# A new order of all engines' work and of all PSUM banks in a fused attention and mixture-of-experts kernel

## The chip, the cores and the metric

The kernel runs on one core of a Trainium2 chip. The metric is the device time of one execution in microseconds. Five engines work side by side, each in its own program order: TensorE (PE: matmuls, transposes; its weight loads are listed apart as PEld), VectorE (DVE), ScalarE (ACT), GpSimd (POOL) and SyncE (SP). They wait for each other through semaphores. Transfers run on 16 DMA engines and are issued here from the queues of GpSimd (the rows' loads), SyncE (stores, small constants) and ScalarE (one weight).

## The reference

Local attention over 8 batches, 8 heads, 576 positions and 64 values per head. Heads 0 to 3 see the last 32 positions, heads 4 to 7 every fourth of the last 128. The result, as 4608 tokens of 512 values, goes through a gated pair of low-rank experts.

```python
scores = scale * np.matmul(q, k.transpose(0, 1, 3, 2))
mask_plain = (rel >= 0) & (rel < 32)
mask_dil = (rel >= 0) & (rel < 128) & (rel % 4 == 0)
attn = softmax(where(mask, scores, -1e9))
x = (attn @ v).transpose(0, 2, 1, 3).reshape(4608, 512)
...
logits = x @ w_gate                     # 8 experts, the best 2 of each token
w = softmax(the two logits)
out = x + sum over the 2 experts of w * ((x @ A[e]) @ B[e])   # rank 16
```

## The kernel before

The host lays q, k and v out so that the dilated heads become plain bands as well (positions sorted by their remainder of 4), and ones are put beside v so that the softmax's sums come out of the same matmul. One batch is one "row", r = 0 to 7; g = 0 are the plain heads, g = 1 the dilated ones.

For each row, in names that the plan uses (a digit for the part, then r, then g):

- **Loads** L, on GpSimd's DMA queue, from f32 to bf16 on the way, into four input slots (row r uses slot r % 4, so row r waits until row r-4 has been used). Rows 2 to 6 are one operation of two DMAs each. Rows 0, 1 and 7 are cut up: Lq7gh are the queries and keys of one group and half, Lv7gh its values.
- **S0, S1** (TensorE): masks, then scores of key blocks 0 to 4 and 5 to 8, 24 and 20 matmuls, into two banks each. **E0, E1** (ScalarE): exponentials into the tile p.
- **V** (TensorE, 26 matmuls, three banks): the values. **R** and **N** (VectorE): reciprocal of the sums and the product with it, into the row x. **B** (GpSimd): x as bf16.
- **T**, **U** (TensorE): transposes of it, **C**, **Cd**, **Cp** (ScalarE) their copies to xt. **Z0, Z1** (TensorE): x times A and the gate, **Y0, Y1** (ScalarE) copies.
- **m0, m1, s12, tt, top, g2** (VectorE) and **th** (ScalarE): the gate's weights from the two largest logits. **gz** (GpSimd, VectorE in row 7): gated products. **G**, **H** (TensorE): their transposes; **gc**, **gn** (ScalarE) copies.
- **D0, D1, D2** (TensorE): products with B. **A0, A1, A2** (VectorE) add them to x; in the last rows a part goes by ScalarE (**dx**, **dy**) and GpSimd (**A3**, **A2**).
- **O** (SyncE): the row's store. Rows 6 and 7 are stored in halves. Every store waits for six of the eight loads of row 7 (Lq700, Lq701, Lq710, Lq711, Lv710, Lv711), and a store of a whole row for the one two before it in the plan.

At the start stand warm and the fillers F0 to F2 (matmuls on a tile of zeros), awf/awc and btf/btc (weights and their casts), con, cc0, cc1 and cd0 to cd3 (the masks), tab (a first exponential), pz, xz and vz (fills with zeros).

The order of everything is a text, PLAN. A word is an operation's name; after an @ stands the first of the PSUM banks that it takes. `Program.ordered` reads it: each engine executes its operations in the order in which they stand there, and an operation that takes a bank waits for all that last used this bank. `Program.run` makes the semaphore waits from these and from the dependencies named in `add(...)`. Neither looks at times.

## Time and profile before

| | |
|---|---|
| median of 3 runs | 101.61 us (101.57 to 102.17) |
| the profiled execution | 101.74 us, span 100.0 us |
| busy in the span: PE, PEld, DVE, ACT, POOL | 81.0, 59.3, 61.6, 72.0, 51.0 us |
| HBM read, written | 29.07 MB, 9.44 MB |
| matmuls | 1585, with as many weight loads |
| mean granted TensorE clock | 0.974 of full speed |

The span goes from the first to the last instruction of the program. In a row of the timeline stand start, length, engine, line, operation, written and read tiles, count, and in brackets the idle time before it and what ended that. A row of the chain has start, length and what. A row of windows has a stretch, its length, busy time and count of PE, PEld, DVE, ACT and POOL, the granted clock, the share of the DMA engines' time and their rate. A row of groups ends with busy time, mean nanoseconds of one, idle time before. "issue" is time in which an engine waited for nothing that the profile shows.

### The profile page before, as it was taken

To read this page: it belongs to the slowest core of one execution; us is meant where nothing else is said; L and a number is where in the kernel's file an instruction comes from. 1 tells how busy PE (TensorE), PEld (TensorE's weight loads), DVE (VectorE), ACT (ScalarE), POOL (GpSimd) and SP (SyncE) were. 2 spreads that over 40 slices of the span, in tenths; PEclk is the share of its full clock that TensorE was granted. 3 is DMA by queue.
4 is the path that set the end of the run, shared out by engine and by line. 5 is a ranking of instruction groups with operands and counts; after the bars stand their busy time and mean duration, and the time that the engine had idled before them with its cause. 6 is when DMAs were issued, how large, how long until landed. Compare 5 with 4: busy or idle time off the path is not lost.

```text
span 100.0 us, 3591 instructions
## 1 busy us (share of the span) xinstructions
PE 81.0 (81%) x1585; PEld 59.3 (59%) x1585; DVE 61.6 (62%) x138; ACT 72.0 (72%) x123; POOL 51.0 (51%) x68
## 2 busy tenths in 40 slices
PE   5999979969874886989886996999999999868300
PEld 3345565547554664669654865887886888745100
DVE  5800068732991458908926498297597399989700
ACT  5643740998986977795699488979989999956300
POOL 5999006915440050852960346749367508666800
PEclk9999999999999999999999999999999999999955
DMA  2999999999999999999999999797889999869994
GB/s 47 310 207 200 213 211 212 223 202 214 213 210 222 209 214 209 213 219 212 213 210 218 209 212 216 127 214 138 153 198 424 428 405 417 364 269 420 420 415 168
DMA packets 5727, 24.50 MB, mean 245 GB/s; under 512 B 720, under 2 KB 848, under 8 KB 4944
## 3 DMA queue, kind: packets, MB, share of 16 engines
q0 software_dynamic: 3840, 14.23, 72.1%
q1 hardware_dynamic: 1728, 9.77, 23.7%
q10 hardware_dynamic: 144, 0.28, 0.9%
q8 instruction: 12, 0.20, 0.8%
q14 instruction: 3, 0.02, 0.1%
HBM read 29.07 MB, written 9.44 MB: 385 GB/s over the span
## 4 chain that ended last, share of the span: by engine, by line
PE 48%; DMA 21%; ACT 13%; DVE 5%; POOL 4%; issue 3%; POOLq 0%
PE ps L212 43%; DMA in<-in_qkv_dram 21%; ACT p L345 8%; PE ps L408 3%; PE ps L498 2%; DVE x L384 1%; POOL x L553 1%; DVE x L545 1%; DVE tt L483 1%; POOL xb L391 1%; ACT xt L418 1%; ACT gn L517 1%; ACT awf L571 1%; POOL x L573 1%; ACT gc L514 1%
## 5 line engine op out<-in xcount | busy, mean ns | idle before, releaser
L345 ACT ACTIVATE p<-ps 128x960 bf16<-128x960 f32 (+1 forms) x32 | 27.7, 891 | 7.6 <-PE ps L212 7.1
L391 POOL CAST xb<-x 128x1152 bf16<-128x1152 f32 (+1 forms) x16 | 17.6, 1111 | 22.0 <-DVE x L384 22.0
L212 PE MATMUL ps<-in,p 128*64 128x130 bf16 (+1 forms) x416 | 21.4, 221 | 1.5 <-ACT p L345 1.5
L384 DVE TENSOR_TENSOR x<-ps,rec 128x1152 f32<-128x1152 f32 x16 | 21.7, 1357 | 0.5
L212 PEld LDWEIGHTS ps<-in,p 128*64 128x64 bf16 (+1 forms) x416 | 17.1, 104 | 4.7 <-ACT p L345 2.1
L545 DVE TENSOR_TENSOR x<-x,ps 128x1024 f32<-128x1024 f32 (+1 forms) x16 | 17.3, 1114 | 1.2 <-PE ps L212 1.2
L381 DVE RECIPROCAL rec<-ps 128x18 f32<-128x18 f32 x16 | 4.3, 271 | 21.8 <-PE ps L212 21.5
L493 POOL TENSOR_TENSOR gz<-zs,g 128x640 bf16<-128x640 f32 x7 | 8.9, 1274 | 16.5 <-DVE g L488 16.5
L212 PE MATMUL ps<-warm 128*128 128x512 f32 x20 | 11.9, 738 | 1.2 <-DVE warm L216 1.2
L272 POOL DMA_DIRECT2D in<-in_qkv_dram x22 | 11.7, 570 | 0.8 <-POOLq L674 0.8
L212 PEld LDWEIGHTS ps<-in 64*64 64x64 bf16 x576 | 10.7, 106 | 2.4 <-issue 0.4
L212 PE MATMUL ps<-in 64*64 64x96 bf16 (+1 forms) x576 | 11.6, 200 | 0.2 <-issue 0.2
L212 PE MATMUL ps<-aw,xt 128*128 128x136 bf16 x160 | 11.2, 223 | 0.7 <-ACT xt L424 0.4
L418 ACT COPY xt<-ps 128x1024 bf16<-128x1024 bf16 x8 | 8.1, 1011 | 4.0 <-PE ps L408 4.0
L408 PE MATMUL ps<-one,xb 128*128 128x128 bf16 x128 | 9.6, 219 | 1.6 <-issue 0.9
L212 PEld LDWEIGHTS ps<-aw,xt 128*128 128x128 bf16 x160 | 9.6, 98 | 1.5 <-ACT xt L424 0.7
L408 PEld LDWEIGHTS ps<-one,xb 128*128 128x128 bf16 x128 | 7.6, 98 | 3.1 <-issue 1.4
L466 ACT COPY zs<-ps 128x408 f32<-128x408 f32 (+1 forms) x14 | 6.1, 443 | 3.3 <-PE ps L212 3.1
L212 PEld LDWEIGHTS ps<-warm 128*128 128x128 f32 x20 | 4.4, 239 | 5.6 <-issue 4.3
L212 PE MATMUL ps<-bt,gc 128*128 128x256 bf16 (+1 forms) x48 | 6.7, 256 | 1.2 <-ACT gc L514 0.7
L421 ACT COPY xt<-ps 128x1024 bf16<-128x1024 bf16 x7 | 7.2, 1022 | 0.6 <-PE ps L408 0.6
L212 PE MATMUL ps<-con,one 64*64 64x480 bf16 (+1 forms) x64 | 5.9, 359 | 2.1 <-DMA in<-in_qkv_dram 1.7
(54 smaller groups left out, 98.1 us busy)
## 6 DMA issues: line engine op xcount, KB each, us to landing
in<-in_qkv_dram POOLq DMA_DIRECT2D x10, 868.5 KB, 17.9
out_dram<-x SPq DMA_DIRECT2D x6, 1152.0 KB, 5.8
in<-in_qkv_dram POOLq DMA_DIRECT2D x10, 288.0 KB, 5.6
out_dram<-x SPq DMA_DIRECT2D x4, 576.0 KB, 3.6
in<-in_qkv_dram POOLq DMA_DIRECT2D x10, 146.2 KB, 7.3
in<-in_qkv_dram POOLq DMA_DIRECT2D x2, 434.2 KB, 13.2
awf<-in_aw_dram ACTq DMA_DIRECT2D x1, 272.0 KB, 3.0
btf<-in_bt_dram SPq DMA_DIRECT2D x1, 256.0 KB, 3.3
```

The lines of the kernel that those rows point to most:

```text
L212: return nc.tensor.matmul(o, lhsT=lhsT, rhs=rhs, start=start, stop=stop, skip_group_check=True)
L272: nc.gpsimd.dma_start(out=IN[r % SLOTS][half(a), at : at + n], in_=qkv[r, a, :, at - 2 * VB * a : at - 2 * VB * a + n],) if n < ROW else n ...
L345: return [nc.scalar.activation(p[:, :, :].rearrange("p h (s c) -> p h s c", c=PER)[:, :, b0 : b0 + nb, 0:SEG], PS[:, k.at : k.at + 2, 0 : ...
L381: rc = add(f"R{tag}", "DVE", ("el", 60), lambda: [nc.vector.reciprocal(rec[:, :].rearrange("p (b i) -> p b i", b=3), PS[:, k.at : k.at + 3 ...
L384: nm = add(f"N{tag}", "DVE", ("el", XG), lambda: [nc.vector.tensor_tensor(X[r][:, XG * g : XG * g + XG].rearrange("p (b i n) -> p b i n", ...
L391: add(f"B{tag}", "POOL", ("el", cut), lambda: [nc.gpsimd.tensor_copy(XB[r % 2][:, g, 0:cut], X[r][:, XG * g : XG * g + cut])], [nm] + free)
L408: nc.tensor.transpose(tp[j][:, 128 * u : 128 * u + 128], xb[:, g, 256 * u + 128 * j : 256 * u + 128 * j + 128], ident())
L418: return [nc.scalar.copy(xt[:, 0:2, 0:S].rearrange("p j (c i) -> p j c i", c=C)[:, :, :, 0:128], tp.rearrange("p j (i c) -> p j c i", c=C))]
L421: return [nc.scalar.copy(xt[:, 2:4, 0:512], tp)]
L466: zc.append(add(f"Y{st}{r}", "ACT", ("el", len(us) * ZW), lambda us=us, k=k: [nc.scalar.copy(zs[:, us[0] : us[-1] + 1].rearrange("p u n -> ...
L493: return [en.tensor_tensor(GZ[i][:, us[0] : us[0] + n, :].rearrange("p u (e r) -> p u e r", e=E), zv()[:, us[0] : us[0] + n, 0:ER].rearran ...
L545: return [nc.vector.tensor_tensor(v, v, PS[:, k.at : k.at + nk].rearrange("p b n -> p (b n)"), ALU.add)]
```

## The change

PLAN is replaced by another order of the same 426 operations with other banks, and the waits of the first copies on ScalarE name tab (which stands before them on the same engine) as well. All operations, their shapes and the rest of their dependencies stay; so does the wait of the stores for six of row 7's eight loads. The new order is the result of a search in which TensorE's instruction fetches were counted.

```diff
-    add("cc0", "ACT", ("el", SEG), ..., ["con"])
+    add("cc0", "ACT", ("el", SEG), ..., ["con", "tab"])
...
-        CON[:, 3 * SEG :]..., ONE[:, 0:SEG]...)], ["con"])
+        CON[:, 3 * SEG :]..., ONE[:, 0:SEG]...)], ["con", "tab"])
...
-                    zeros(i, a).bitcast(FP), WARM[...]...)], ["wz"])
+                    zeros(i, a).bitcast(FP), WARM[...]...)], ["wz", "tab"])
```

The text before:

```
con awf btf wz tab cc0 pz1 pz0 Lk00 cc1 vz21 vz00 Lk01 xz0
vz01 warm@7 cd3 Lv00 xz1 cd2 S100@1 pz3 cd0 Lv01 L11 S000@5 E000 F0@4
btc cd1 L10 E100 S001@6 S101@4 V00@1 E101 awc L2 E001 V01@5 R00 F1@0
N00 B00 T00@4 C00 R01 F2@3 N01 B01 U0@6 Cp0 Cd0 T01@7 C01
L3 L4 S111@2 S011@0 Z00@7 E011 Y00 Z10@0 vz10 vz11 Y10 pz2 m00 m10
s120 E111 S110@6 S010@4 top0 tt0 th0 g20 E110 gz0 E010 V11@0 R11 N11
G0@7 V10@3 B11 R10 gc0 N10 gn0 D02@7 D00@0 B10 A02 T11@6 vz20 D01@2
vz30 C11 U1@7 Cd1 Cp1 T10@4 A00 C10 S121@0 E121 A01 Z11@2 Y11 m11
Z01@7 Y01 S021@5 m01 top1 E021 S020@3 S120@1 s121 tt1 th1 g21 gz1 E020
V21@5 E120 G1@3 R21 gn1 V20@0 gc1 N21 D12@3 R20 D11@6 vz31 A12 N20
S030@4 B20 E030 D10@0 S130@2 E130 S131@4 E131 B21 A11 A10 S031@6 E031 L5
U2@0 T21@5 V30@1 Cd2 T20@4 R30 C21 N30 B30 V31@5 Cp2 R31 N31 L6
C20 Z12@0 Y12 Z02@1 Y02 m02 m12 s122 S141@2 E141 S140@5 E140 T30@7 S041@1
tt2 th2 E041 B31 U3@0 S040@5 C30 V41@1 Cd3 Cp3 top2 g22 gz2 G2@0
E040 gn2 gc2 R41 N41 T31@4 V40@5 D22@3 R40 A22 N40 C31 Z03@0 Z13@2
Y03 m03 Y13 S150@3 m13 s123 D20@0 E150 S151@6 E151 S051@4 D21@2 top3 tt3
th3 B41 B40 A20 T41@7 E051 g23 A21 gz3 U4@1 T40@0 C41 Lq700
Lq711 Lq701 S050@2 Lv710 Cp4 V51@5 R51 N51 Cd4 G3@1 E050 V50@2 R50 N50
C40 gn3 Z14@0 gc3 B51 Y14 Z04@5 Y04 S060@0 B50 D30@6 E060 S160@4 Lq710
E160 Lv711 Lv701 S161@2 E161 D32@1 Lv700 A30 T50@0 S061@6 A32 C50 m14 m04
top4 V60@1 s124 tt4 T51@4 th4 U5@0 E061 V61@5 O0 R60 N60 O1 S170@2
Cp5 g24 C51 Cd5 Z05@1 E170 R61 Z15@4 Y05 Y15 gz4 N61 G4@0 B60
gn4 D31@6 m05 gc4 B61 S070@2 E070 S171@4 A31 m15 T60@0 top5 E171 s125
tt5 th5 g25 S071@6 O2 O3 V70@1 R70 T61@4 E071 C60 V71@5 U6@0 N70
C61 Cp6 D42@1 Cd6 dx4 gz5 G5@4 D40@2 Z06@1 A42 R71 N71 gn5 gc5
A40 D41@6 A41 B70 Bx7 Y06 Z16@4 Y16 m06 D52@0 dx5 U7@1 B71 Cd7
T70@2 m16 O4 s126 Cp7 T71@3 C70 D50@0 A52 top6 D51@5 tt6 Cx7 th6
C71 Z07@2 Z17 g26 A50 A51 gz6 dy5 m07 G6@7 gc6 m17 s127 tt7
th7 top7 A53 O5 g27 gz7 gy7 D61@0 gn6 A61 D62@5 dx6 A62 O61
D60@6 dy6 A63 G7@2 H7 gn7 D70@5 gc7 gm7 D72@3 dx7 A72 A60 O60
D71@1 A70 A71 D73@6 dy7 A73 O71 O70
```

The text after:

```
awf wz con warm@5 awc F0@4 btf btc Lk00 pz3 tab cc0 S100@0 cc1
Lk01 cd1 S000@5 Lv00 vz20 vz01 vz00 vz10 pz1 cd2 cd3 F1@7 xz1 vz30
Lv01 vz21 L11 L10 vz11 pz0 pz2 E100 E000 L2 cd0 S001@3 E001 S101@0
E101 V00@5 R00 N00 V01@2 B00 T00@7 R01 C00 S111@0 S011@5 N01 B01 U0@3
T01@2 Cp0 C01 Cd0 xz0 Z00@2 E111 E011 Z10@7 Y00 m00 S010@3 Y10 m10
S110@5 V11@0 top0 s120 tt0 E010 R11 th0 E110 g20 L3 N11 V10@3 R10
N10 gz0 B11 G0@6 gn0 T11@7 gc0 D00@0 A00 F2@2 vz31 B10 U1@6 C11
Cd1 T10@2 S020@0 Cp1 C10 E020 S121@5 E121 D01@2 Z11@4 Y11 A01 L4 Z01@1
Y01 m01 S120@5 S021@3 D02@7 A02 E120 E021 V20@0 m11 top1 s121 tt1 th1
g21 R20 V21@3 N20 gz1 G1@0 gc1 R21 N21 B20 S130@1 gn1 E130 S131@3
D11@6 A11 S030@1 E131 B21 S031@3 E030 T21@5 V30@0 R30 T20@6 U2@7 N30 C21
E031 V31@3 R31 N31 C20 Cp2 Cd2 Z12@1 Y12 Z02@0 Y02 D10@6 A10 S141@2
E141 S140@4 L5 m02 E140 S041@0 E041 S040@6 B30 m12 s122 tt2 th2 T30@3
E040 D12@2 A12 B31 T31@4 L6 top2 U3@5 Cp3 g22 V41@0 Cd3 C31 C30
R41 N41 gz2 V40@5 G2@4 gc2 gn2 Z13@3 R40 N40 Z03@2 Y03 m03 Y13
m13 D20@0 Lq711 B41 A20 Lq710 s123 B40 Lv711 S150@6 E150 S051@2 D21@4 A21
E051 S151@6 E151 S050@0 E050 tt3 th3 T41@2 C41 top3 V51@3 g23 gz3 R51
N51 B51 T40@7 U4@6 C40 V50@0 Cp4 Cd4 G3@7 R50 Z14@3 gc3 gn3 Y14
Z04@5 T51@4 Y04 N50 D30@6 Lq701 Lq700 B50 C51 S160@0 S060@2 A30 m04 E160
S161@4 S061@6 E060 D22@0 m14 top4 E161 s124 A22 Lv710 tt4 th4 V60@1 g24
E061 R60 N60 U5@4 Lv701 T50@0 Cd5 Cp5 V61@5 O1 R61 C50 S171@3 Z05@2
D31@0 N61 E171 O2 A31 Y05 Z15@4 Y15 m05 m15 s125 tt5 S170@6 S070@2
S071@4 D32@1 gz4 O0 E170 top5 G4@0 Lv700 E070 A32 th5 E071 g25 B61
T61@6 C61 V70@1 gc4 B60 T60@4 gz5 R70 N70 B70 gn4 C60 V71@5 G5@1
U6@0 D40@3 R71 N71 B71 A40 Cp6 Cd6 Z16@0 D42@2 gc5 gn5 D41@6 Y16
A41 dx4 Z06@0 Bx7 A42 O3 Y06 D52@4 U7@1 T71@2 Cp7 T70@7 m06 D51@5
dx5 Cd7 m16 O4 C71 s126 top6 tt6 Cx7 A52 th6 D50@0 C70 Z07@2
Z17 g26 dy5 gz6 A51 G6@5 A50 m07 gc6 m17 s127 D61@0 tt7 A53
O5 th7 gn6 D62@7 top7 g27 dx6 gz7 gy7 A61 A62 D60@5 dy6 O61
A63 G7@3 H7 gc7 gn7 gm7 A60 D70@7 A70 O60 D72@0 dx7 D73@3 D71@1
A71 A72 O71 dy7 A73 O70
```

## The prediction

> **What bounds the kernel now.** I read the page first, for the span and for the two rates of the transfers.

> ```profile
> span 100.0 us, 3591 instructions
> PE 81.0 (81%) x1585; PEld 59.3 (59%) x1585; DVE 61.6 (62%) x138; ACT 72.0 (72%) x123; POOL 51.0 (51%) x68
> GB/s 47 310 207 200 213 211 212 223 202 214 213 210 222 209 214 209 213 219 212 213 210 218 209 212 216 127 214 138 153 198 424 428 405 417 364 269 420 420 415 168
> q8 instruction: 12, 0.20, 0.8%
> ```

> No engine is full over the whole span. The GB/s row has a plateau near 212 while the rows are loaded, three dips between 62 and 73 us, and a plateau near 420 while they are stored. Next came the chain that ended last, and TensorE's own timeline where that chain leaves a transfer.

> ```profile
> 18.55 21.30 DMA in<-in_qkv_dram
> 39.84 0.04 issue
> 39.89 0.72 PE ps L212 x24
> ...
> 53.00 0.42 PE ps L498 x5
> 53.43 0.94 issue
> 54.36 0.62 PE ps L408 x8
> ...
> 60.04 0.51 issue
> ...
> 76.75 0.25 issue
> ...
> 86.84 1.36 PE ps L212 x20
> ...
> 93.91 1.26 POOL x L553
> ```

> ```profile
> 31.26 0.36 PE L212 MATMUL ps<-con,one 64*64 64x384 bf16 x4 [1.37 <-DMA in<-in_qkv_dram]
> 48.33 0.36 PE L212 MATMUL ps<-con,one 64*64 64x384 bf16 x4 [0.36 <-DMA in<-in_qkv_dram]
> ```

> Up to 48.33 us the landings of L2, L3 and L4 hold the scores of rows 2, 3 and 4: transfers set the pace. From there the chain is compute, and in it are three idles of TensorE (0.94, 0.51, 0.25 us) whose releaser is "issue": all data was there and no instruction was. Cutting the trace at the places where these end shows what they are:

> ```profile
> 48.33:54.36 6.03, 4.52 (x129) 3.33 (x130) 3.54 (x12) 5.54 (x11) 3.27 (x4) 1.00 1.06 214
> 54.36:60.54 6.18, 5.66 (x127) 4.32 (x127) 4.56 (x13) 4.32 (x8) 2.29 (x2) 1.00 1.06 215
> 60.54:66.93 6.39, 6.08 (x126) 5.32 (x127) 4.11 (x7) 5.28 (x9) 4.28 (x6) 1.00 0.94 180
> 66.93:71.46 4.53, 4.48 (x132) 3.39 (x131) 2.97 (x11) 4.30 (x7) 3.37 (x6) 1.00 0.83 146
> 71.46:77.00 5.54, 5.29 (x130) 4.40 (x128) 4.74 (x9) 4.91 (x10) 3.45 (x3) 1.00 0.94 274
> ```

> Columns: stretch, length, busy time and count of each engine, clock, DMA share, GB/s. There are about 127 matmuls with their 127 weight loads between one "issue" idle and the next, twice that between the second and third. 3170 such instructions and q8's 12 packets of 0.20 MB make 64 bytes each and 256 to a packet. So TensorE's program arrives in blocks of 127 pairs, and the block after next is ordered when a block has been left. A block therefore can't be run through faster than a fetch takes: 6.03 and 6.18 us where loads run at 214 GB/s, 5.54 where stores begin, and at most 4.53 where the loads' queue was nearly empty (146 GB/s). Counting matmuls in the program, boundaries fall at the matmuls 730 (S141), 857, 984, 1111, 1238, 1364 and 1491.

> [...]

> **The change, part by part.** Nothing is added or taken away but waits on tab, which stands ahead of their copies on ScalarE anyway: 0. All work, the 1585 matmuls among it, has a new order and new banks.

> *Start.* ScalarE now does btc and three zero fills ahead of the first exponential, and VectorE does four fills ahead of pz0.

> ```profile
> btf<-in_bt_dram SPq DMA_DIRECT2D x1, 256.0 KB, 3.3
> L262 ACT COPY in<-warm 64x1170 f32<-64x1170 f32 x4 | 4.6, 1165 | 0.0
> L260 DVE MEMSET in<- 64x1170 uint32 x4 | 4.1, 1033 | 1.0 <-issue 1.0
> 9.11 0.97 ACT L345 ACTIVATE p<-ps 128x960 bf16<-128x960 f32 x1 [2.86 <-PE ps L212]
> ```

> With btf at some 4.4 us (issued 1.1), btc, the constants and three fills of 1.165 end near 9.9; on VectorE awc ends near 4.2, four fills of 1.03 with their gaps and two short ones bring pz0 to 10.4. E100 starts there, 1.3 us after the first exponential of before (9.11), and with its bank goes S101, so the values of row 0 end some 0.9 us later. The 1.37 us for which TensorE waits for L2 in the row above hides this; without that cover it would cost 0.9.

> *Loads.* L4 moves from behind L3 to behind B10 on GpSimd's queue (near 29.7 us by the same chain), and still has L3 ahead of it, whose landing before was at 39.84. S141 then starts at 48.3 as before; 730 matmuls precede it in both orders. Row 7's loads are spread between B41, B40, B51, B50 and gz4, where they stood in two fours:

> ```profile
> 62.15 2.14 POOL L272 DMA_DIRECT2D in<-in_qkv_dram  x4
> 68.67 2.06 POOL L272 DMA_DIRECT2D in<-in_qkv_dram  x4
> 73.77 0.89 SPq L586 DMA_DIRECT2D out_dram<-x  x2
> in<-in_qkv_dram POOLq DMA_DIRECT2D x10, 868.5 KB, 17.9
> ```

> The first three now go behind gz2 and row 4's casts, at 53 to 59 us, so the dips of the GB/s row close. A row is two loads of 868.5 KB, 8.2 us at 212 GB/s: behind L4's landing at 48.3, L6 lands near 64.6. The six loads that stores wait for make 83% of row 7 (64 x 2304 and 64 x 1170 values each, four and two of four and four), so they land 6.8 us later, at 71.4, and the first stores leave 2.3 us sooner than 73.77. I cost this at 0: the last stores wait for A53 to A73, late compute, and the GB/s row already falls to 269 near 88 us for want of finished rows.

> *From 48.3 us, the fetches.* E141, E140 and E041 run one after the other, then V41:

> ```profile
> 48.98 1.51 ACT L345 ACTIVATE p<-ps 128x768 bf16<-128x768 f32 x2 [0.47 <-PE ps L212]
> 50.66 0.95 ACT L345 ACTIVATE p<-ps 128x960 bf16<-128x960 f32 x1
> 51.66 1.34 PE L212 MATMUL ps<-in,p 128*64 128x130 bf16 x26 [0.45 <-ACT p L345]
> L384 DVE TENSOR_TENSOR x<-ps,rec 128x1152 f32<-128x1152 f32 x16 | 21.7, 1357 | 0.5
> ```

> In the new order V41 can start near 51.45 and reaches matmul 857, its 24th of 26, at 52.65. The block before it began at 48.35 as before, under the same loads, so its instructions come at 54.4 again: 1.7 us of idle in place of 0.94, and V41, R41 and N41 behind it. N41 then ends at 56.3 and N40, behind it on VectorE at 1.36 us with its reciprocal, at 58.0. Boundary 984 is the second matmul of S050, which waits for A20 and so for N40, four maxima and itself: 60.1, and the block comes at 60.5, as before. To 1111 (D30) the order runs T41, V51 (1.34, to 62.9), T40 and U4 (63.6), V50, and G3 behind C40's 1.01 us of copying (65.2); gc3 and gn3 behind G3 let D30 start near 66.8: 66.9, before's 66.93. Gain so far: none.

> The next block is 3 matmuls of D30, four scores, D22, V60, U5 and half of T50. Before ran through 127 in 4.53 us, and this one would take as long (by its work, 71.4). But the load queue, empty before, is now full until 72. Between 4.53 and 6.18 I take the middle, 5.4: 72.3, against 71.46. From 1238 to 1364 (S071) the stretch has T50, V61, S171, Z05, D31, Z15, S170, S070, and at 5.54 ends at 77.8, against 77.00: **+0.8 us**, with bounds of 0 (4.53, then 5.54) and +2.2 (6.18 twice).

> *ScalarE at the end.* Before did gn4 and gc4 ahead of that boundary; after has them behind C61.

> ```profile
> 75.50 0.65 ACT L517 COPY gn<-ps 128x576 bf16<-128x576 bf16 x1
> 76.03 0.66 ACT L514 COPY gc<-ps 128x576 bf16<-128x576 bf16 x1
> ...
> 79.30 1.01 ACT L418 COPY xt<-ps 128x1024 bf16<-128x1024 bf16 x1
> 81.44 0.27 ACT L442 COPY xt<-ps 128x128 bf16<-128x128 bf16 x1 [0.21 <-PE ps L432]
> ...
> 86.21 0.57 ACT L424 COPY xt<-ps 128x512 bf16<-128x512 bf16 x1
> ```

> From 79.30 to the end of Z07's last operand (86.78) ScalarE had one idle, 0.21: this stretch is its own, 7.48 us. Two copies more make 8.6 at their pitch (0.65 less 0.1 of overlap). It starts with C61, behind D32, G4 and T61, 1.7 us after boundary 1364, where before's started 2.3 after it: 10.3 against 9.78 us, 0.5 more. The new stretch also waits for U6 (it stands behind G5, and G5 behind N70) and for Z06 (behind Y16's bank), up to 0.65. I take **+0.8**, bounds +0.5 and +1.15.

> *Tail.* From Z07 on the work is the same in nearly the same order, 8.3 us from 86.84 to A73's end. O5 can leave some 2.0 us after Z07's start:

> ```profile
> 89.18 0.33 SPq L586 DMA_DIRECT2D out_dram<-x  x1
> ```

> That was 2.34 before. O5 with the four half rows is 3.5 MB, 8.4 us at 420 GB/s, and ends the span: **-0.3**.

> Sum, against the profiled execution: 101.74 + 0.8 + 0.8 - 0.3 = 103.0 us. It had 100.0 of span and 1.74 around it, and stands 0.13 above the median of 101.61; the runs spread by more than that, so I leave it at 103.0.

> **The rivals.** *Fetches don't hold the new order* (faster): blocks come within 4.53 us wherever needed, as in the fourth stretch. Then 857 passes at 52.9, V41 is hardly cut, V40 follows at once (its copies are done at 52.8), the values of row 5 run up to 3 us sooner than before's, and 1364 comes at 74.0. From there ScalarE alone sets the pace, at up to +1.15: -3.0 + 1.15 - 0.1 = -1.95, 99.8 us. For it: the row of 4.53. Against it: 6.03 and 6.18, at the very places and loads that the new order meets first.

> *Only the first two boundaries hold* (no change): 1238 at 71.4, 1364 at 76.9, hence -0.1 + 0.8 - 0.3 = +0.4, 102.1. For it: the fourth and fifth row once more. Against it: no gap is left in the loads at 67 to 72 us.

> *Every block at 6.18* (slower still): 66.9, 73.1, 79.2: +2.2 + 1.15 - 0.3, 104.8. For it: the second row. Against it: the fifth, 5.54 with stores running. It decides from the point at which L reaches 6 us behind 66.9.

> *The earlier stores pay*: were the end bound by transfers, 2.3 us sooner would give 99.4. Against it stands 269 in the GB/s row: the queue ran dry near 88 us. I give it nothing of its own; with the first rival it is about the same time.

> **How the numbers follow.** The forecast (102.6 to 104.3) has 0.47, the first rival 0.25, the second 0.20, the third 0.08. About 1% is what a measurement can tell from no change here, 100.6 to 102.6. So faster by over 1% is 0.25, within it 0.20, slower 0.55. The range, 99.6 to 104.4, holds the forecast's own (102.6 to 104.3), the second rival and somewhat over half of the first, and leaves the third out: 0.8 or a little more.

> **What would show it.** Right: TensorE idles for "issue" by some 1.7 us inside V41 near 53 us; again in T50 near 71 and in S071 near 77; the DMA share stays over 1 from 62 to 71 us; the first store leaves near 71.5; ScalarE has hardly an idle from C61 to C70; Z07 starts near 88.1 and A73 ends near 96.4. Wrong: no idle for "issue" over 0.3 behind 61 us, V71 starting ahead of the 79.95 below, or Z07 ahead of 86.84. An early store that also finishes early, with the end still at 98, would make the last rival right. Idle for loads at 31 and 48 us gone would say that the start cost more than its cover.

> ```profile
> 79.95 1.34 PE L212 MATMUL ps<-in,p 128*64 128x130 bf16 x26
> ```

## The result, and the profile after

The changed kernel takes 105.53 us (median of 4 runs, 104.89 to 106.33) against 101.81 us for the one before: a ratio of 1.037, 95% interval 1.028 to 1.045. It is slower, which was the likeliest outcome, but by 3.7 us where 1.3 were forecast, and outside the range. Two later groups of runs of the same kernel gave 1.020 (1.012 to 1.028) and 1.021 (1.014 to 1.027). These ratios take only the runs within 1.5% of the quickest of a group, which are all four here, but three of seven and three of six in the later groups, where the others took 105.14 to 107.61 us. So its time itself varies, and what makes it vary is part of the answer.

The page of the kernel after; for the clock, the row of the kernel before follows in a fence of its own:

```profile
span 104.5 us, 3595 instructions
PE 83.4 (80%) x1585; PEld 62.1 (59%) x1585; DVE 61.5 (59%) x138; ACT 71.2 (68%) x123; POOL 51.1 (49%) x68
PEclk9999999999999589999999579999999999999995
...
GB/s 72 267 175 198 208 211 217 214 211 217 211 214 212 214 214 215 213 204 216 211 215 200 207 214 212 166 9 132 198 121 417 423 419 275 436 250 395 393 413 160
```

```profile
PEclk9999999999999999999999999999999999999955
```

The work is the same, but TensorE is busy 2.4 us longer, and its granted clock falls to a half twice (the 5s near 34 and 58 us) where before it never did ahead of the last 5 us. In the GB/s row the dips are still there, and one is deep: 9 GB/s from 67.9 to 70.5 us. The plateau of the stores begins at 78 instead of 75 us.

The windows of after, cut at the boundaries of the prediction (730, 857, 984, 1111, 1238, 1364) and at the start of Z07. At 730, 1111 and 1364 the cut is the start of the operation that holds the boundary (S141, D30, S071), 0.16 to 0.23 us ahead of the matmul itself:

```profile
51.20:57.29 6.09, 4.33 (x133) 3.48 (x133) 2.53 (x11) 5.48 (x9) 4.04 (x5) 1.00 1.06 209
57.29:64.22 6.93, 6.92 (x124) 5.82 (x127) 4.97 (x12) 3.27 (x7) 3.21 (x4) 0.75 1.05 211
64.22:70.36 6.14, 6.02 (x147) 5.43 (x136) 4.80 (x9) 5.75 (x12) 3.02 (x4) 1.00 0.57 113
70.36:75.61 5.25, 4.42 (x131) 3.23 (x128) 3.38 (x14) 5.00 (x10) 3.65 (x5) 1.00 0.90 159
75.61:80.22 4.61, 4.61 (x123) 3.92 (x127) 3.60 (x5) 2.75 (x5) 1.78 (x4) 1.00 0.79 239
80.22:91.68 11.46, 10.26 (x187) 8.02 (x175) 9.84 (x28) 10.97 (x23) 6.32 (x8) 1.00 0.93 386
```

Cut at matmul 1364 itself (80.45), as in the kernel before, the last two windows are 4.84 and 11.23 us long.

With the same cuts in the kernel before, in the forecast (its terms added to before's stretches), and in fill_l2, an experiment below in whose profile the clock never halves before the end, the spans divide like this:

| stretch (us) | before | forecast | after | fill_l2 |
|---|---|---|---|---|
| start to 730 (S141) | 48.33 | 48.3 | 51.20 | 49.02 |
| 730 to 1111 (D30) | 18.60 | 18.6 | 19.16 | 18.84 |
| 1111 to 1238 (T50) | 4.53 | 5.4 | 5.25 | 6.15 |
| 1238 to Z07 | 15.38 | 16.2 | 16.07 | 16.07 |
| Z07 to the end of A73 | 8.33 | 8.0 | 7.99 | 7.99 |
| A73 to the end | 4.83 | 4.8 | 4.83 | 4.53 |
| span | 100.0 | 101.3 | 104.5 | 102.6 |

TensorE's timeline of after, at the two long idles and behind them:

```profile
32.84 0.40 PE L212 MATMUL ps<-one 64*64 64x480 bf16 x4 [1.99 <-DMA in<-in_qkv_dram]
...
34.34 2.47 PE L212 MATMUL ps<-aw,xt 128*128 128x136 bf16 x20
...
54.36 1.17 PE L212 MATMUL ps<-in,p 128*64 128x130 bf16 x23
57.30 2.37 PE L212 MATMUL ps<-in,p 128*128 128x130 bf16 x29 [1.76 <-issue]
...
75.61 0.45 PE L408 MATMUL ps<-one,xb 128*128 128x128 bf16 x5 [0.60 <-issue]
```

V41 is cut behind its 23rd matmul, with 1.76 us of "issue", as forecast; T50 idles 0.60; in S071 there is none. Z11 and Z01 (20 matmuls) take 2.47 us, and the end of V41 with V40 (29) takes 2.37. Windows of 3.41 us laid at the clock records show why:

```profile
30.52:33.93 3.41, 1.42 (x53) 1.05 (x50) 0.05 (x1) 2.04 (x5) 0.79 (x2) 1.00 1.07 217
33.93:37.34 3.41, 3.41 (x44) 2.93 (x45) 1.22 (x1) 2.19 (x4) 0.00 (x0) 0.50 1.06 213
54.41:57.83 3.42, 1.66 (x34) 1.28 (x36) 0.35 (x2) 2.92 (x5) 1.81 (x2) 1.00 1.03 201
57.83:61.24 3.41, 3.41 (x41) 3.23 (x36) 2.98 (x4) 1.00 (x2) 1.61 (x2) 0.50 1.05 212
```

A window in which TensorE was busy for 42 and 49% is followed by one at half the clock. The length of 3.41 us is that of the trace's own records of the granted clock: in after they last 27.31, 3.41, 20.48, 3.41, 40.96 and, the last, 4.37 us, and the first five are 8, 1, 6, 1 and 12 times 3.41.

The first of these stretches lies ahead of S141, where after lost most: 2.87 us. In the kernel before, S141 waited for the landing of L4 (the row with 0.36 in the prediction). In the chain of after no transfer stands in front of it from 38 us on; last come the values V31, the reciprocal R31 and the product N31:

```profile
47.98 1.36 PE ps L212 x26
49.36 0.28 DVE rec L381
49.66 1.37 DVE x L384
51.17 1.77 PE ps L212 x80
```

L4 had landed at 49.49, 1.68 us ahead of S141 (before: 48.29). S141 waits for N31 through a bank: V31 takes the banks 3 to 5 now and S141 the banks 2 and 3, where V31 had 5 to 7 before. So time lost ahead of V31 is no longer hidden by the wait for a load. Of the 13 profiles with this order here (those that change the masks aside), seven have no halved clock ahead of S141, and there it starts 0.07 to 0.34 us behind the landing of L4; in the six that have one it starts 0.26 to 2.95 us behind.

Then the loads and stores: GpSimd's and SyncE's timelines of after.

```profile
68.61 1.14 POOL L391 CAST xb<-x 128x1152 bf16<-128x1152 f32 x1 [0.68 <-DVE x L384]
69.69 1.08 POOL L272 DMA_DIRECT2D in<-in_qkv_dram  x2
```

```profile
77.01 16.92 SPq L586 DMA_DIRECT2D out_dram<-x  x6
```

Lq701 and Lq700 stand behind the cast B51, which waited for its x, and were issued at 69.69, when the queue had already been empty. The first store left at 77.01, not at 71.5.

Last, the chain that ended last in after, from T50 to Z07:

```profile
75.61 0.45 PE ps L408 x5
76.07 4.00 PE ps L212 x90
...
80.09 1.67 ACT p L345 x2
...
81.98 1.33 PE ps L212 x26
...
85.16 0.44 PE ps L498 x5
85.60 0.11 PE ps L432 x2
...
91.68 1.36 PE ps L212 x20
```

Row 7's first values (V70, at 81.98) wait for exponentials, and these for the scores S170, which now stand behind Z05, D31 and Z15. (S170 also shares a bank with N61, but N61 ended at 79.05 and S170 started at 79.44, right behind Z15; TensorE has no idle from T50 to boundary 1364.) G5 (85.16, L498) waits for N70 with its bank, and U6 (L432) stands behind G5. By the two timelines V70 starts 1.2 us behind boundary 1364 before and 1.5 after, U6 4.1 and 5.0. The rest is lost at Z07. The first row below is after's, the second before's, the third ScalarE in after:

```profile
91.68 1.36 PE L212 MATMUL ps<-aw,xt 128*128 128x136 bf16 x20 [0.97 <-ACT xt L418]
```

```profile
86.84 1.36 PE L212 MATMUL ps<-aw,xt 128*128 128x136 bf16 x20 [0.40 <-ACT xt L424]
```

```profile
90.49 0.24 ACT L485 ACTIVATE th<-tt 128x40 f32<-128x40 f32 x1 [0.30 <-DVE tt L483]
```

TensorE waits 0.97 us for C70, which is now the last copy and stands behind th6, for which ScalarE waits 0.30 us; before, it waited 0.40 us for C71.

### The profile page after: what moved, and what is told of

Its sections match the earlier page's. It is cut to its first block, busy times and chain, and to the rows that moved or that the text cites. A ratio compares the mean times of both kernels' runs of the same rounds, so it can differ in the third digit from the quotient of the medians.

```text
span 104.5 us, 3595 instructions
## 1 busy us (share of the span) xinstructions
PE 83.4 (80%) x1585; PEld 62.1 (59%) x1585; DVE 61.5 (59%) x138; ACT 71.2 (68%) x123; POOL 51.1 (49%) x68
## 3 DMA queue, kind: packets, MB, share of 16 engines
HBM read 29.07 MB, written 9.44 MB: 368 GB/s over the span
## 4 chain that ended last, share of the span: by engine, by line
PE 36%; DMA 23%; ACT 16%; POOL 9%; DVE 7%; issue 4%; POOLq 0%
PE ps L212 30%; DMA in<-in_qkv_dram 23%; POOL in L272 7%; ACT p L345 6%; PE ps L408 3%; DVE x L384 3%; DVE x L545 2%; PE ps L498 2%; ACT gn L517 2%; ACT xt L421 2%; ACT gc L514 2%; ACT zs L466 2%; POOL x L553 1%; ACT xt L418 1%; DVE tt L483 1%
## 5 line engine op out<-in xcount | busy, mean ns | idle before, releaser
L345 ACT ACTIVATE p<-ps 128x768 bf16<-128x768 f32 (+1 forms) x32 | 27.2, 901 | 5.2 <-PE ps L212 5.1
L212 PE MATMUL ps<-in,p 128*64 128x130 bf16 (+1 forms) x416 | 22.2, 225 | 3.5 <-issue 1.8
L212 PEld LDWEIGHTS ps<-in,p 128*64 128x64 bf16 (+1 forms) x416 | 17.7, 106 | 7.3 <-ACT p L345 2.6
L384 DVE TENSOR_TENSOR x<-ps,rec 128x1152 f32<-128x1152 f32 x16 | 21.7, 1358 | 0.5
L212 PE MATMUL ps<-aw,xt 128*128 128x136 bf16 x160 | 12.9, 242 | 2.2 <-ACT xt L438 1.3
L212 PEld LDWEIGHTS ps<-aw,xt 128*128 128x128 bf16 x160 | 11.4, 108 | 3.4 <-ACT xt L438 1.6
L212 PE MATMUL ps<-warm 128*128 128x512 f32 x20 | 12.0, 751 | 1.2 <-DVE warm L216 1.2
L272 POOL DMA_DIRECT2D in<-in_qkv_dram x22 | 11.7, 575 | 0.8 <-POOLq L674 0.8
L212 PEld LDWEIGHTS ps<-in 64*64 64x64 bf16 x576 | 10.8, 108 | 2.0
L408 PE MATMUL ps<-one,xb 128*128 128x128 bf16 x128 | 9.8, 219 | 2.7 <-POOL xb L391 2.1
L212 PE MATMUL ps<-in 64*64 64x96 bf16 (+1 forms) x576 | 11.5, 202 | 0.0
L418 ACT COPY xt<-ps 128x1024 bf16<-128x1024 bf16 x8 | 8.2, 1030 | 4.2 <-PE ps L408 4.2
L408 PEld LDWEIGHTS ps<-one,xb 128*128 128x128 bf16 x128 | 7.5, 98 | 3.5 <-POOL xb L391 2.5
L514 ACT COPY gc<-ps 128x576 bf16<-128x576 bf16 x7 | 4.5, 647 | 7.0 <-PE ps L498 7.0
L212 PEld LDWEIGHTS ps<-warm 128*128 128x128 f32 x20 | 4.6, 243 | 6.3 <-issue 5.0
L212 PE MATMUL ps<-one 64*64 64x384 bf16 (+1 forms) x64 | 6.1, 369 | 2.0 <-DMA in<-in_qkv_dram 2.0
## 6 DMA issues: line engine op xcount, KB each, us to landing
in<-in_qkv_dram POOLq DMA_DIRECT2D x10, 868.5 KB, 16.3
btf<-in_bt_dram SPq DMA_DIRECT2D x1, 256.0 KB, 3.1
```

What stands on the lines that cost most here:

```text
L212: return nc.tensor.matmul(o, lhsT=lhsT, rhs=rhs, start=start, stop=stop, skip_group_check=True)
L272: nc.gpsimd.dma_start(out=IN[r % SLOTS][half(a), at : at + n], in_=qkv[r, a, :, at - 2 * VB * a : at - 2 * VB * a + n],) if n < ROW else n ...
L345: return [nc.scalar.activation(p[:, :, :].rearrange("p h (s c) -> p h s c", c=PER)[:, :, b0 : b0 + nb, 0:SEG], PS[:, k.at : k.at + 2, 0 : ...
L384: nm = add(f"N{tag}", "DVE", ("el", XG), lambda: [nc.vector.tensor_tensor(X[r][:, XG * g : XG * g + XG].rearrange("p (b i n) -> p b i n", ...
L408: nc.tensor.transpose(tp[j][:, 128 * u : 128 * u + 128], xb[:, g, 256 * u + 128 * j : 256 * u + 128 * j + 128], ident())
L418: return [nc.scalar.copy(xt[:, 0:2, 0:S].rearrange("p j (c i) -> p j c i", c=C)[:, :, :, 0:128], tp.rearrange("p j (i c) -> p j c i", c=C))]
```

## The experiments

Each compares with the kernel before on the same chip; the interval in brackets is 95%. As the changed kernel alone gave 1.020 to 1.037, ratios between these tell little from each other. What decides is the stretches of the profiles, each of one execution.

**start: the zero fills back at their places.**

```diff
- wz awc vz01 vz00 vz10 pz1 vz11 pz0 pz2 (VectorE)   btc ... vz20 ... vz30 ... E100 (ScalarE)
+ wz pz1 pz0 vz00 vz01 pz3 awc ... vz10 vz11 pz2     ... E101 btc vz20 vz30
```

> The new order with the zero fills and btc at the start put back near where the old order has them; nothing else moves. Theory S (the fills of 5 to 10 us slow the loads, 185 against 203 GB/s in that stretch): L2 lands near 31.3 instead of 32.8, TensorE's wait for it falls from 2.0 to under 1 us, so no half clock at 34 us either, and S141 starts near 48.5: 2 to 3 us less than the new order, 102.5 to 103.5. Rival (the late L2 is chance, or comes from the order of the loads): L2 lands at 32.8 again and the time stays within 0.5 us of the new order's.

Measured: 1.020 (1.017 to 1.023). S141 starts at 48.39 us; but with the new start it was 48.12 (few_loads), 48.62 (fill_both) and 49.06 (again), and with before's 48.33 and 48.90 (end_mix). L2 landed at 31.36 here, and at 31.20 to 32.15 in all other profiles of this order but after's own, so the 32.80 there was chance. A cost of the fills on the loads isn't seen. Whether the new start makes a halved clock in the first rows likelier stays open: in five of the 12 profiles with it the clock halves between 14 and 22 us, in this one not, and between 10 and 22 us in one of the four with the kernel before's order up to there (before_loads).

**fill_l2: the filler F2 moved to where TensorE waits for L2.**

```diff
- A00 F2@2 vz31 ... T10@2 S020@0
+ A00 vz31 ... T10@2 F2@3 S020@0
```

> The new order with the filler F2 (one f32 matmul on zeros, 1.0 us) moved from ahead of U1 to ahead of S020, into TensorE's wait for L2. Theory C (an idle of some 2 us halves the clock for 3.4 us): the half clock at 34 to 37 us is gone, D01, Z11, Z01 and S120 take 0.6, 0.65, 0.87 and 0.5 us instead of 0.85, 1.11, 1.57 and 0.78, V20 starts 1.6 us sooner, and the time falls by 1.3 to 1.7 us. Rival (these four are slow through contention, or the slow clock isn't on the path): they stay as they are, or the time stays within 0.4.

Measured: 1.024 (1.018 to 1.030). No halved clock ahead of the end. The 20 matmuls of Z11 and Z01, and the two idles, in its timeline:

```profile
33.57 1.35 PE L212 MATMUL ps<-aw,xt 128*128 128x136 bf16 x20
...
55.31 1.61 PE L212 MATMUL ps<-in,p 128*128 128x130 bf16 x29 [1.95 <-issue]
74.01 0.45 PE L408 MATMUL ps<-one,xb 128*128 128x128 bf16 x5 [1.62 <-issue]
```

1.35 instead of 2.47 for the 20 matmuls: that is the price of the clock. The two idles for "issue" stay, and the ratio is no lower than that of the later groups of after.

**fill_v41: a filler ahead of V41.**

```diff
- FILL = (("S000", 2), ("V01", 2), ("S111", 1),)
+ FILL = (("S000", 2), ("V01", 2), ("S111", 1), ("V41", 2),)
- g22 V41@0
+ g22 F3@2 V41@0
```

> The new order with one more filler (two f32 matmuls, 1.9 us) ahead of V41. Theory F (V41's 24th matmul waits for an instruction block): V41 starts 1.9 us later and still ends near 57.7; TensorE isn't idle there, so the clock stays whole at 58 to 61 us, V40, G2, Z13 and Z03 take 1.34, 0.44, 0.64 and 0.87 us, and the time falls by 0.7 to 1.3 us. Rival (V41 is held by something else): V41 ends 1.9 us later and the time rises by 1 to 2 us.

Measured: 1.023 (1.015 to 1.030). V41 starts 5.05 us behind the start of S141, where it started 3.2 us behind it without the filler, and it ends 7.32 us behind it, where it ended 6.3 to 7.2 us behind. Its end is set in the main by the fetch, not by its start.

**loads: row 7's last five loads right behind Lv711.**

```diff
- Lv711 S150@6 ... D30@6 Lq701 Lq700 ... Lv710 ... Lv701 ... Lv700
+ Lv711 Lq701 Lq700 Lv710 Lv701 Lv700 S150@6 ... D30@6
```

> The new order with the last five loads of row 7 issued right behind Lv711 instead of behind B51, B50 and gz4. The loads' queue doesn't run dry at 68 to 70 us, the six land near 73.3 and the first store leaves there instead of at 77.0. Theory T (the late stores are a bound of their own beside the compute): 0.5 to 1 us less than the new order. Rival (compute alone sets the end): within 0.3 of it. Rival (a full load queue slows the instruction fetches at 70 to 76 us): 0.5 us or more slower, with a longer idle in T50.

Measured: 1.043 (1.036 to 1.050). The prediction's stores came, and the kernel got no faster:

```profile
71.80 2.33 SPq L586 DMA_DIRECT2D out_dram<-x  x2
```

```profile
74.39 0.45 PE L408 MATMUL ps<-one,xb 128*128 128x128 bf16 x5 [1.52 <-issue]
81.23 0.37 PE L212 MATMUL ps<-in 64*64 64x96 bf16 x17 [1.85 <-issue]
```

The first store leaves 5.2 us sooner than in after, and S071, which had no idle there, waits 1.85 us for its instructions.

**again: the changed kernel itself.**

> The changed kernel once more, as a measure for the others of this group and for the TensorE clock. If the halved clock hangs on where a free-running window of 3.41 us falls on the two idles of 1.8 to 2.0 us, then in this profile the idles stand at the same places (ahead of S020, inside V41) but the halved stretches can differ: with one of them gone V40 takes 1.3 instead of 2.1, or D01 0.6 instead of 0.85. If the drops belong to the order itself, both come again at 34 and 58 us. The late landing of L2 (32.80) should be nearer 31.5 if it was chance; then time 104.5 to 105.3, else 105.5 again.

Measured: 1.020 (1.012 to 1.028). The idle in V41 is there (1.90), the halved clock behind it is not: V40 takes 1.33 us, where it took 2.09 in the first profile. Over the 13 profiles in which V41 is cut, V40 took 1.33 or 1.34 eight times and 2.09 to 2.28 five times. A window busy for 54% (51.57 to 54.98) kept the clock. Of the windows at full clock ahead of 90 us in the 18 profiles, each of the 13 busy for up to 48.5% was followed by half the clock, none over 53% was, and between them it went both ways. Of the windows already at half clock, the four busy for 62.7 to 82.4% (in act_short, again2 and tail_both) were followed by half the clock again, those from 86.3% on by the full one. Over the 13 runs of this group and of again2 the times go from 103.50 us at a mean clock of 0.974 to 107.61 us at 0.913.

**masks and before_masks: two mask matmuls of 128 rows for four of 64.**

```diff
- for pr, a, c in tiles:
-     mm(PS[half(c), k.at + pr, 0 : nb * SEG], ident(a), mask(a), True, False)
+ for pr in range(2):
+     mm(PS[:, k.at + pr, 0 : nb * SEG], ident(), mask(), True, False)
```

> After, with each mask written by two matmuls of 128 rows in place of four of 64, the same values: 64 matmuls fewer in the program (1521), no other work. If TensorE is held by the fetch of its program, the 857th matmul is now in Z13 and no longer in V41: V41 runs through in 1.34 us, its 1.8 us of idle go, the halved clock after it too, and from S141 to S071 some 28 matmuls fewer at 6 us for 127 save 1.0 to 1.5 us: time 103.5 to 104.3. If the idle in V41 is a wait of its own (for a bank or for p) it stays at the 24th of its 26 matmuls, and the time stays at that of after, 105 to 105.5.

> The kernel before, with the same two mask matmuls in place of four (1521 matmuls). By the fetch theory the 857th, 984th and 1111th matmul fall on Z03, V51 and S161 instead of T31, D21 and S060; the issue idles of 0.94 and 0.51 us shrink or move, and the time falls by 0.7 to 1.4 us, to 100.5 to 101.1. If the number of instructions doesn't matter: 101.5 to 102.

Measured: 1.061 (1.056 to 1.067) and 1.040 (1.034 to 1.047), both against every expectation, as the edit was not neutral. The groups of masks, then one of the two of after (the other has 5.9):

```profile
L212 PE MATMUL ps<-con,one 128*128 128x480 bf16 (+1 forms) x32 | 8.6, 349 | 0.8 <-DVE x L384 0.4 <-ACT con L240 0.2
L212 PE MATMUL ps<-one 128*128 128x384 bf16 (+1 forms) x32 | 8.5, 348 | 0.0
```

```profile
L212 PE MATMUL ps<-one 64*64 64x384 bf16 (+1 forms) x64 | 6.1, 369 | 2.0 <-DMA in<-in_qkv_dram 2.0
```

17.1 us of busy time for 64 full masks against 12.0 for 128 quarter masks (11.8 in the kernel before). But the place of the stall is shown. Here matmul 857 lies in Z13, and V41 and V40 run as one piece without an idle:

```profile
55.13 2.61 PE L212 MATMUL ps<-in,p 128*64 128x130 bf16 x52
```

V41's data, banks and neighbours were the same. What held it was the count of instructions ahead of it. Z13 doesn't idle in its place: with the longer masks TensorE is busy for all of the 5.75 us up to it (52.46 to 58.21). In before_masks no idle for "issue" over 0.2 us is left, and the kernel is slower all the same.

**act_short: row 4's two gate copies cut short.**

```diff
- nc.scalar.copy(GC[i][:, :], bank(k).bitcast(BF)[:, 0:S])
+ nc.scalar.copy(GC[i][:, 0:n], bank(k).bitcast(BF)[:, 0:n])     # n = 16 for row 4, and gn alike
```

> After, with row 4's two copies of the gates (gc4 and gn4, 576 columns each) cut to 16 columns; the rest of GC and GN keeps row 2's values, so row 4 of the output is not that of the reference. If ScalarE alone sets the time from C61 to Z07, Z07 comes 0.8 to 1.1 us sooner after boundary 1364 (10.4 to 10.7 instead of 11.46 us) and the time falls as much below that of after. If something else holds Z07 (U6, Z06, VectorE), it gives 0.3 or less.

Measured: 1.031 (1.024 to 1.039), and 16.07 us from 1238 to Z07 (75.04 to 91.11), as in after. ScalarE's timeline:

```profile
82.94 0.21 ACT L514 COPY gc<-ps 128x16 bf16<-128x16 bf16 x1
83.00 0.22 ACT L517 COPY gn<-ps 128x16 bf16<-128x16 bf16 x1
83.22 1.01 ACT L418 COPY xt<-ps 128x1024 bf16<-128x1024 bf16 x1
85.17 0.27 ACT L442 COPY xt<-ps 128x128 bf16<-128x128 bf16 x1 [0.94 <-PE ps L432]
```

The 0.8 us that the two copies gave back turned into 0.94 of waiting for U6. ScalarE alone does not set this stretch; my theory of it fell.

**few_loads: the traffic taken away.** The five later loads of row 7 are cut to 64 columns.

```diff
- [(h, QK_AT[h][g], QK)]             [(h, V_AT[h][g], VB)]
+ [(h, QK_AT[h][g], QK if g else 64)]   [(h, V_AT[h][g], VB if g * h else 64)]
```

> After, with the five later loads of row 7 (Lq701, Lq700, Lv710, Lv701, Lv700) cut to 64 columns each, at their places; row 7 then works on what row 3 left in the slot, so its part of the output is not that of the reference. 2.1 MB of loads between 68 and 77 us are gone. If the traffic of the loads makes a fetch of TensorE's program slow, the block from matmul 1111 to 1238 passes in 4.4 to 4.7 us (its work, as in the kernel before, where the queue was dry) instead of 5.0 to 6.2, and T50 has no issue idle; the time falls 0.6 to 1.5 us below that of after. If the fetch takes its time whatever the traffic, it stays at 5.0 to 6.2 and the time changes by less than 0.4.

Measured: 1.037 (1.024 to 1.049), the profiled execution 103.42 us; the windows from 1111 to 1238 of few_loads and of again, one fence each, and TensorE's row in S071 of few_loads:

```profile
66.99:71.30 4.31, 4.03 (x126) 3.09 (x127) 2.60 (x12) 4.02 (x6) 2.33 (x4) 1.00 0.28 48
```

```profile
67.61:73.76 6.15, 4.25 (x127) 3.14 (x128) 4.21 (x13) 4.84 (x9) 4.09 (x6) 1.00 0.87 152
```

```profile
77.97 0.37 PE L212 MATMUL ps<-in 64*64 64x96 bf16 x17 [1.54 <-issue]
```

The same block takes 4.31 us with a DMA share of 0.28 and 6.15 with 0.87, and T50's idle is gone. The stores then leave at 70.3, and S071 idles 1.54: the gain is given back there. The fetches themselves stand in the traces, as packets of 16 KB of queue q8. The one ordered at boundary 1111 starts 1.0 us behind it here (68.13) and 3.7 us behind it in again (71.47); in before and after one starts behind each of the seven boundaries from 730 on, by 1.8 to 3.8 and by 1.1 to 4.3 us. At every idle for "issue" over 0.2 us behind 30 us, in all profiles, TensorE goes on 1.2 to 1.8 us behind the end of such a packet.

**before_loads: the reverse, on the kernel before.**

```diff
- gz2 ... B41 B40 ... Lq700 Lq711 Lq701 S050@2 Lv710 ... Lq710 ... Lv711 Lv701 ... Lv700
+ gz2 Lq700 ... B41 Lq711 B40 Lq701 Lv710 Lq710 Lv711 Lv701 Lv700 ... S050@2
```

> The kernel before, with Lq700 moved behind gz2, Lq711 behind B41 and row 7's other six loads behind B40, so that the dips of the load rate at 62 to 73 us close; the first stores then leave near 71.5 instead of 73.77. If traffic slows the fetches, the block from 1111 to 1238 takes 5.2 to 6.2 us instead of 4.53, the next one over 5.54 as stores run in it, and the time rises by 0.7 to 2 us. If the fetch doesn't care and early stores pay, it is the same or up to 0.5 us less.

Measured: 1.025 (1.012 to 1.038).

```profile
68.27:74.50 6.23, 4.43 (x131) 3.31 (x127) 4.50 (x14) 4.77 (x7) 1.18 (x2) 1.00 0.80 173
```

The block that took 4.53 us takes 6.23 with as much work (4.43 busy). Filling the dips of the load rate made the kernel before slower.

**fill_both: both fillers.** The edits of fill_l2 and fill_v41 together.

> After, with the filler F2 moved to just ahead of S020 and a new one (one matmul on zeros, 0.9 to 1 us) ahead of V41, where TensorE idles. No data wait, bank or fetch is taken away. If the halved clock is what spreads and lifts the times of after (103.5 to 107.6), no 3.41 us window is under half busy, the clock is never halved before the last 8 us, and the times lie within 103.3 to 104.3. If the clock has little to do with it, they spread as those of after do, round 105.

Measured: 1.033 (1.025 to 1.041), with times of 104.39 to 107.19 us: not the 103.3 to 104.3 expected, and spread as those of after are. The clock did not halve in its profile, but T50's block came late (1.62 us of idle). So the clock explains single profiles; that it explains the whole spread is not shown.

**tail_before: after up to C50, then before's order and banks.**

```diff
- C50 S171@3 Z05@2 D31@0 ... S170@6 S070@2 ... G4@0 ... E071 ... C61 V70@1 gc4 ... V71@5 G5@1 U6@0
+ C50 S170@2 g24 Z05@1 E170 ... G4@0 B60 gn4 D31@6 ... gc4 ... S070@2 ... V71@5 U6@0 ... G5@4
```

> After up to C50 (T50, V61), and from there the order and banks of before (S170@2 ahead of S171, G5@4 behind U6, gn4 and gc4 ahead of E070), with D32 and A32 behind D31 and A31 and Lv700 ahead. If the end of after is long because S170 waits for N61 and G5 for N70, both through banks, the stretch from boundary 1238 to Z07 falls from 16.07 to 15.4 us and the time by 0.7 us. If it is ScalarE's two copies that were moved, V70 starts no sooner and C61 to C70 alone shrinks, by about 1.0. If the fetch of block 1364 holds it anyway (T60 or S071 stalls), 0.3 or less.

Measured: 1.022 (1.012 to 1.032), the span of its profile 101.4 us. The windows from 1238 to 1364 and on to Z07:

```profile
73.46:78.50 5.04, 5.03 (x122) 4.17 (x126) 3.85 (x7) 3.70 (x7) 2.72 (x3) 1.00 0.85 289
78.50:88.42 9.92, 9.42 (x181) 7.91 (x173) 8.64 (x25) 9.87 (x21) 4.60 (x6) 1.00 0.96 395
```

14.96 us in place of 16.07. As shortening the two copies alone gave nothing (act_short), this points to the order and banks: S170 behind Z15, G5 behind N70, and C70 behind th6. V70, U6 and Z07 start 1.2, 4.1 and 9.9 us behind 1364 here, as in the kernel before, and Z07 waits 0.40 us again. Which of the three has how much was not tried one by one. The ratio is no lower than that of after in its later groups, so the gain in this stretch isn't seen in the time.

**stores_late: all stores behind S071 as well.**

```diff
- + more + late)
+ + more + late + ["S071"])
```

> After, with all stores waiting for the scores S071 as well (O1 and O2 stand behind it in the order), so that no store runs before about 79 us. If stores in front of it make the fetch of the block from 1364 late (1.5 and 2.6 us of issue idle in S071 where the first store left at 70.3 and 71.8, none where it left at 76 or 77), the stretch from 1238 to 1364 is 4.6 to 4.8 us and S071 has no issue idle; Z07 then comes 16.0 us behind 1238. The time is 0.5 to 1.5 us below that of after if nothing else binds. If the end is bound by the transfers, 9.44 MB at 420 GB/s from 79 us on land near 102 us, and it is the same or up to 1 us more.

Measured: 1.061 (1.056 to 1.067), far more than expected.

```profile
74.94:79.54 4.60, 4.60 (x123) 3.91 (x127) 2.77 (x4) 2.75 (x5) 1.11 (x2) 1.00 0.26 36
```

No idle in S071, Z07 16.06 behind 1238: as the fetch theory says, but no better than after, whose stores were late enough. The end is now the transfers': they start at 80.31 and the last lands at 105.7. In the five profiles whose first store leaves ahead of boundary 1238 (few_loads, loads, before_loads, masks, before_masks) the fetch ordered there starts 2.9 to 4.8 us behind it, and four of them idle 0.35 to 1.85 us at the next boundary; in the other 13 it starts 1.0 to 3.3 us behind, and the idle is 0.25 us at most. So stores may leave neither ahead of that boundary nor as late as here.

**again2, tail_both, end_mix.** The changed kernel once more; tail_before with after's order from Z07 on; the kernel before with after's order from Z07 on.

```diff
- C71 Z07@2 Z17 g26 A50 A51 gz6 dy5 m07 G6@7 ... (before)
+ C71 Z07@2 Z17 g26 dy5 gz6 A51 G6@5 A50 m07 ... (after)
```

> The changed kernel once more, for comparison with the others of this group. By the fetch theory, the profile has issue idle in V41; in T50 by the load rate near 70 us; and in S071 only if the first store leaves ahead of about 75 us. Time 104 to 105.5.

> After up to C50, then the order and banks of before up to C71 (as in tail_before), and from Z07 on those of after. If the two ends add up, Z07 comes 14.9 to 15.4 us behind boundary 1238 and A73 ends 8.0 instead of 8.33 us behind Z07: 0.3 us below tail_before, 1.0 to 1.4 below after. If O5 or the stores hold the end, no gain on tail_before.

> The kernel before up to C71, and from Z07 on the order and banks of after: a version that could be a little faster than both. A73 should end 8.0 instead of 8.33 us behind Z07, and the time fall by 0.3 us, to 0.997 of before; if the stores set the end, or G6 waits for its new bank, no change.

Measured: 1.021 (1.014 to 1.027), 1.019 (1.013 to 1.025) and 0.996 (0.987 to 1.006). In again2 T50 idles 0.27 and S071 not at all, with the first store at 76.19. From Z07 to the end of A73 tail_both and end_mix take 8.08 us, against 8.33: a quarter of a microsecond, too little to be told from no change in the time. tail_both has 14.96 us from 1238 to Z07 in its profile, but its time is not the 1.0 to 1.4 us below after that was expected.

## Why the prediction was right or wrong

- **The direction was right, and so was the account of the fetches; the largest loss was not in the sum.** TensorE's program comes in blocks (12 packets of 16 KB in the span; in before and after one starts behind each boundary from 730 on), and the new order meets their boundaries at worse places. V41 idles 1.76 us near 55 (1.7 near 53 forecast), masks shows that the instruction count decides where (V41 and V40 in one piece once 857 lies in Z13), and few_loads and before_loads that the traffic decides how long (4.31 us for a block at a DMA share of 0.28, 6.23 at 0.80). No run bore out the first rival, that fetches don't hold. But of the 4.5 us by which after's span is longer, 2.87 lie ahead of S141, where the forecast had none.
- **"S141 then starts at 48.3 as before": the step that failed most.** The prediction took the landing of L4 for what S141 waits for, and the loads for a cover of all that stands ahead. S141 started at 51.17. L4's landing accounts for 1.20 of it (49.49 for 48.29; L2's late landing, 32.80 for 31.22, was chance). The other 1.68 are the chain to N31, whose bank S141 now takes. Ahead of that chain the halved clock, which stands in no term of the sum, took 1.6 us from S020 to S021 (32.84 to 37.37, against 32.26 to 35.19 in fill_l2). In fill_l2, without it, S141 starts at 48.99. An order with V31 on banks apart from S141's was not run. (724 matmuls stand ahead of S141 in the new order and 728 in the old, not 730 in both; that is at most 0.2 us.)
- **The clock behind V41.** It took up to 0.85 us from 857 to 984 (6.93, against 6.08 in again). The idle of 1.7 us in V41, which I had costed at nothing up to 1111, had a price: the window it fell into.
- **The fourth block hangs on the queue.** I took 5.4 us for 1111 to 1238 as a middle, and in after it took 5.25. Counted from matmul 1111 itself it took 4.8 to 5.7 us in seven profiles of this order, after's among them, and 6.0 to 6.1 in five. few_loads and before_loads show what decides: 4.31 us where the loads are cut (48 GB/s, a DMA share of 0.28), 6.23 where they are moved ahead (173 GB/s, 0.80).
- **The fifth was sized too high.** I passed on before's 5.54 us; it took 4.84, its own work, with no idle in S071.
- **ScalarE at the end: the step failed, and its size was too low.** From 1364 to Z07 after takes 11.23 us against 9.84: 1.39 more, where I had 0.8. ScalarE's two copies were not the reason (act_short). I had U6 behind G5 and N70 as a small addition; U6 came 0.9 us later, and the wait for C70 behind th6, which I did not have, added 0.6 at Z07. Only because the fifth block's error went the other way does 1238 to Z07 come out near the forecast (0.69 for 0.8): luck.
- **Loads and stores: the step failed.** I moved three of eight loads and took the dips for closed, without asking when B51, ahead of the other five on GpSimd's queue, would get its x. The six landed at 76.87 instead of 71.4. And costing earlier stores at nothing was wrong even so: in loads and few_loads they came with an idle of 1.5 to 1.9 us in S071.
- **The tail was right.** From Z07 to A73 0.34 us were won where 0.3 were forecast.

By the ratios of the later groups (1.020 and 1.021) about 2.1 of the 3.7 us of the first result come again. That the rest is the halved clock and the late loads is argued from the profile of after, not shown. In size the prediction's terms had 1.3 of the 2.1. In fill_l2, whose span is 1.3 us above the forecast's, they lacked 0.96 us up to 1111 and 0.75 at T50 (1.62 for 0.87), and had 0.4 too much behind it. No version of the new order brought the time back to that of before, so the causes are shown for the stretches, and for the time as a whole they stay open.

## What to carry to other kernels

Where an engine's program is long, find the boundaries of its blocks by counting instructions between "issue" idles, and ask of each what the DMA queues hold when the next block is ordered: load that fills a dip elsewhere may be paid for there, as in before_loads (6.23 us for a block of 4.53). An idle can cost more than its length: 20 matmuls behind a window of 3.41 us busy for 42% took 2.47 us in after, and 1.35 in fill_l2, where a filler stood in the idle. So two orders with equal sums need not be equal if one has the longer single gaps. A wait for a load covers what stands ahead of it only as long as no bank ties the waiting operation to a chain of its own. Before naming an engine as the bound of a stretch, shorten its work there: if the freed time turns into a wait, the bank or the operation that it waits for is the bound.
